# Three pairs of token blocks instead of two in the seven-product tail of an attention and feed-forward kernel; early activations parked in DRAM

## The chip, the cores and the metric

The kernel runs on one core of a Trainium2 chip. The metric is the device time of one execution in microseconds (us); lower is better. Three runs of the kernel before are shown, and one further execution was taken with the hardware profiler on.

## What is computed

The reference chains a thresholded attention and a feed-forward block with a quick GELU. All arrays are float32, except that the two weight matrices arrive as float64.

```python
# q, k, v: (8, 8, 576, 64)
scores = scale * np.matmul(q, k.transpose(0, 1, 3, 2))
thresh = np.max(scores, axis=-1, keepdims=True) - tau
scores = np.where(scores >= thresh, scores, -1000000000.0)
attn = np.exp(scores - np.max(scores, axis=-1, keepdims=True))
attn_out = np.matmul(attn / (np.sum(attn, axis=-1, keepdims=True) + 1e-09), v)
x = attn_out.transpose(0, 2, 1, 3).reshape(4608, 512)
h = x @ w_in                                  # w_in: (512, 2048)
g = h * (1.0 / (1.0 + np.exp(-1.702 * h)))
out = g @ w_out                               # w_out: (2048, 512)
```

## The kernel before, in words

**Attention.** 8 batches of 4 pairs of heads make 32 "pairs" n = 0 to 31. For a pair, TensorE computes transposed scores, 36 matrix products of 64x288 (`scores_run`, L538). ScalarE copies them out of PSUM (`keep`, L555), VectorE takes maxima (`in_groups`, L561) and folds them into a row (L570, L581, L594, L605), and two DMAs on the SP queue send that row to DRAM and bring it back spread over the partitions (`row_out` L651, `row_in` L660). VectorE subtracts it (`sub`, L666), ScalarE masks and exponentiates (L672, L676), VectorE sums (L561 again), the sums go the same way through DRAM (`sums_out` L754, `sums_in` L761), TensorE multiplies by the values (`values`, L687, 36 products of 64x288), and VectorE writes the normalised result into a transposed activation tile (`place_x`, L789). From pair 7 on, the value products of pair n-2 and the score products of pair n are interleaved in one run of 72 products.

**Feed-forward.** The 4608 tokens form 18 blocks of 256. Blocks 0 and 1 are done together in a plain way (L844, L826). Blocks 2 to 13 (`feed_forward`) have a plain first product, `mm1` at L804: 64 products of 128x256 to a block. GELU is a tanh on ScalarE (L813) and one VectorE instruction (L816). The second product is always made by the Strassen-Winograd scheme of seven half-size products (`second` and `product`, L995: 56 products of 128x256 to a block), with its sums on GpSimd (`s_sums`, `s_last`) and its readout on VectorE (L1017). The last four blocks, `TAIL = NBLK - 4`, go in two pairs through `two_blocks`, where the first product too is made of seven half-size ones (`product1`, L909: 112 products of 128x256 to two blocks where `mm1` has 128). That needs sums of weights (`w_sum`, L883) and of activations (`x_sum`, L892). The weight sums lie in `arena2`, in which the scores of the attention live, so the tail can only begin when the attention has ended.

**Storage of x.** A block's transposed activations take one of `NXT = 5` tiles `xT` of 128x1024 floats. `place_x` of a batch's first pair opens the tiles of its new blocks, and waits if none is free; the last first-product of a block frees its tile.

**What sets the order.** Nothing is ordered by hand. The kernel describes its work as tasks (engine, estimated cost, rank, predecessors, buffers taken and given). `run_in_order` plays them through on these costs and writes the instructions of each engine in the order in which it starts them. Attention tasks are ranked by pair number plus a bias for each function. All TensorE tasks of the feed-forward have the lowest rank (`LAST`), so they fill what the attention leaves free. A gate holds them together: the scores of pair n may start only when the feed-forward task of number `per_pair * (n - LEAD)` is done, with `per_pair = 16` and `LEAD = 6`. A plain block is 31 such tasks. [...]

```python
    for n in range(NP):
        gate = per_pair * (n - LEAD)
        after = [ffn[gate]] if gate >= 0 and ffn else []
```

Of the kernel before, what the change touches and what calls it, by code (L numbers as in the profile page):

```python
# [10 lines left out]
FP32 = mybir.dt.float32  # L11
# [8 lines left out]
P = 128  # L20
# [10 lines left out]
def kernel(  # L31
# [34 lines left out]
    nc = tc.nc  # L66
    B, H, S, D = q.shape
# [7 lines left out]
    BLK = 256  # L75
    BANK = 512
    HT = BLK // 2
    HF = d_ff // P // 2
    HM = d_model // 2
    NBLK = B * S // BLK  # L80
    NDC = d_model // P
    NFC = d_ff // P
# [5 lines left out]
    const = ctx.enter_context(tc.tile_pool(name="const", bufs=1))  # L88
    work = ctx.enter_context(tc.tile_pool(name="work", bufs=2))
    dram = ctx.enter_context(  # L90
        tc.tile_pool(name="dram", bufs=2, space=bass.MemoryType.DRAM)
    )
# [33 lines left out]
    NXT = 5  # L126
# [105 lines left out]
    def task(engine, cost, rank, f, *a, after=(), take=(), give=(), lag=None):  # L232
        if lag is None:
            lag = LAG[engine]
        if 0 <= rank < LAST:
            biases = EARLY if a[0] < NPAIR else SECOND if a[0] < 2 * NPAIR else LATER
            rank += CV[f.__name__] if f.__name__ in CV else biases.get(f.__name__, 0.0)
        tasks.append((engine, cost, rank, f, a, [x for x in after if x is not None],
                      take, give, lag))
        return len(tasks) - 1  # L240

    FIRST, LAST = -9.0, 1000.0
# [7 lines left out]
    def transfer(by, time, a, kind=0, give=(), lag=1.7):  # L250
        return task(by, time, FIRST, moved, kind, after=[a], give=give, lag=lag)
# [520 lines left out]
        nc.vector.transpose(out=rc, in_=r.unsqueeze(2).to_broadcast([P, QB, 32]))  # L772
        rcs[n] = rc

    xTs = {}

    def cuts(b):

        return sorted({0, SH, S} | {x for x in range(-b * S % BLK, S, BLK)})

    def place_x(n):
        b, hp = divmod(n, NPAIR)
        rc, pv = rcs.pop(n), pvs.pop(n)
        for a, z in zip(cuts(b), cuts(b)[1:]):
            blk, off = divmod(b * S + a, BLK)
            if blk not in xTs:
                xTs[blk] = work.tile([P, NDC, BLK], FP32, name="xT", tag="xT", bufs=NXT)
            c = a // SH
            nc.vector.tensor_tensor(  # L789
                out=xTs[blk][:, hp, off : off + z - a],  # L790
                in0=pv[:, c, a - c * SH : z - c * SH], in1=rc[:, a:z], op=ALU.mult,
            )
# [7 lines left out]
    def mm1(blk, j, f):  # L800
        if f == 0:
            hidden[j] = psM.tile([P, BANK], FP32, name="hps", tag="mo")
        for c in range(NDC):
            nc.tensor.matmul(  # L804
                hidden[j][:, ts(f, BLK)],
                lhsT=w_in[:, c, ds((f * HF + j) * P, P)], rhs=xTs[blk][:, c, :],
                start=(c == 0), stop=(c == NDC - 1),
            )


    def tanh(j):
# [28 lines left out]
    def mm1_0(j, i):  # L840
        if i == 0:
            hidden[j] = psM.tile([P, BANK], FP32, name="hps", tag="mo")
        for c in range(NDC):
            nc.tensor.matmul(  # L844
                hidden[j][:, ts(i, BLK)], lhsT=w_in[:, c, ts(j, P)], rhs=xTs[i][:, c, :],
                start=(c == 0), stop=(c == NDC - 1),
            )

    def gelu_0(j):
        nc.vector.scalar_tensor_tensor(  # L850
# [4 lines left out]

    TAIL = NBLK - 4
    WQ = NDC // 2 * HF * P
    gx_o = 4 * WQ  # L860
    xs_o = gx_o + N_G
# [36 lines left out]
    def product1(blk, j, x):  # L898
        b11, b12, b21, b22 = (x_quarter(blk, d, h) for d in range(2) for h in range(2))
        left, right = (  # L900
            (wq[0][0], b11), (wq[0][1], b21), (wc[1], xsum[1]), (wc[2], b12),
            (wq[1][1], xsum[2]), (wc[0], xsum[0]), (wc[3], b22),
        )[x]
        if BANK_OF[(7 * j + x) % 5] == "psA":
            places[j, x] = psA.tile([P, 2, 512], FP32, name="ps", tag="ps")[:, 0, 0:BLK]
        else:
            places[j, x] = psM.tile([P, BANK], FP32, name="ops", tag="mo")[:, 0:BLK]
        for c in range(2):
            nc.tensor.matmul(  # L909
                places[j, x], lhsT=left[:, c, ts(j, P)], rhs=right[:, c, :],  # L910
                start=(c == 0), stop=(c == 1),
            )

    def read1(j, x):
        (c11, c12), (c21, c22) = ([hs[j % 2][:, f, h, :] for h in range(2)] for f in range(2))
# [112 lines left out]
    NP = B * NPAIR  # L1028
# [173 lines left out]
    def two_blocks(blk):  # L1202

        b = -(-(blk + 1) * BLK // S) - 1
        xs = [placed[n] for n in range(NP)]
        first, xd = not done_w, []
        for x in range(4):
            if first:
                done_w.append([task("DVE", 0.61, LAST - 1.0, w_sum, x, 0, nc.vector, after=done_w[-1:][0] if done_w else xs)])
            after = (xd[-1:] or xs) + (done_w[x][:1] if first else []) + last_product1  # L1210
            xd.append(task("DVE", 0.61, LAST - 1.0, x_sum, blk, x, after=after))
        if first:
            for k in range(1, HF // 2):
                for x in range(4):
                    after = xs + done_w[x - 1][-1:] + done_w[x][-1:]
                    done_w[x].append(
                        task("POOL", 1.35, FIRST, w_sum, x, k, nc.gpsimd, after=after)
                    )
        last_product1.clear()
        g1, sums = {}, []  # L1220
        for j in range(HF):
            reads = [None] * 7
            for x in range(7):

                after = ffn[-1:] + [placed[n] for n in range(NPAIR * (b + 1))]
                if x in (P6, P7, P5, P3):
                    after += [done_w[{P6: 1, P7: 2, P5: 0, P3: 3}[x]][j // 2]]
                if x in (P6, P7, P4, P5):
                    after += [xd[{P6: 1, P7: 2, P4: 3, P5: 0}[x]]]
                if x == P3 or first:  # L1230
                    after += xs
                bank = (BANK_OF[(7 * j + x) % 5],)
                ffn.append(task(
                    "PE", FFU / 2, LAST, product1, blk, j, x, after=after, take=bank,
                    give=("xT", "xT") if x == P3 and j == HF - 1 else (),
                ))
                if x == P1:
                    a = task("ACT", 0.3, FIRST, read1, j, x, after=ffn[-1:], take=("hs",), give=bank)
                else:
                    a = task(  # L1240
                        "DVE", 0.67 if x == P5 else 0.335, FIRST, read1, j, x,
                        after=ffn[-1:] + reads, give=bank,
                    )
                reads[x] = a
            for h in range(2):
                a = task("ACT", 0.48, FIRST, tanh1, j, h, after=[reads[P5 if h == 0 else P3]], take=("io",))
                g1[j, h] = task(
                    "DVE", 0.65, FIRST, gelu1, j, h, after=[a, last_mm2.get(j // 4), g1.get((j, 0))],
                    give=("io", "hs") if h else ("io",),
                )  # L1250
            if j % 2:
                sums.append(task(
                    "POOL", 2.3, FIRST, s_sums, j // 2, after=[g1[j - 1, 0], g1[j, 0]]
                ))
        last_product1.extend(ffn[-1:])
        second(blk, 0, {j: [g1[j, 0]] for j in range(HF)}, sums)

        again = [g1[j, 1] for j in range(HF)]
        a = task("DVE", 1.14, FIRST, s_sum1, 0, after=again + ffn[-3:-2])
        b = task("DVE", 1.14, FIRST, s_sum1, 1, after=[a] + ffn[-1:])  # L1260
        c = task("DVE", 1.14, FIRST, s_sum1, 2, after=[b])
        second(blk + 1, 1, {j: [g1[j, 1]] for j in range(HF)}, [[a], [b], [c]])
# [1 line left out]
    gelus = {}  # L1264
    next_blk = 0

    per_pair = 16
    lvs = []
    exped, loaded, summed = {}, {}, {}

    def valued(n, pv):

        nonlocal next_blk
        b, hp = divmod(n, NPAIR)
        new = {(b * S + x) // BLK for x in cuts(b)[:-1]} if hp == 0 else set()
        if b:
            new -= {(b * S - 1) // BLK}
        placed[n] = task(
            "DVE", 1.05, float(n), place_x, n, after=[summed[n], pv], take=("xT",) * len(new),
            give=("psA", "rc"),  # L1280
        )
        while hp == NPAIR - 1 and (next_blk + 1) * BLK <= (b + 1) * S:
            if next_blk >= TAIL:
                if (next_blk - TAIL) % 2:
                    two_blocks(next_blk - 1)
            elif next_blk >= PLAIN:
                feed_forward(next_blk)
            elif next_blk == PLAIN - 1:
                first_blocks()
            next_blk += 1  # L1290

    for n in range(NP):
        gate = per_pair * (n - LEAD)
        assert gate < len(ffn) or gate <= 0
# [197 lines left out]
```

## Time and profile before

| quantity | value |
|---|---|
| three runs | 1310.16, 1313.54 and 1313.73 us; median 1313.54 us |
| profiled execution, its own time | 1311.6 us |
| its span, first to last instruction | 1309.8 us (1.8 us lie around it) |
| mean granted TensorE clock | 0.989 of full speed |
| TensorE matmul busy | 1260.5 us |
| VectorE busy | 1002.2 us |
| ScalarE busy | 646.6 us |
| GpSimd busy | 246.1 us |
| last value products of the attention (pair 31) start | 1073.01 us |
| first `product1` of the tail starts | 1112.60 us |

The trace records a float32 matrix product as two matmul records, so "x4" in a line of TensorE is two products. Busy is the time in which at least one instruction of the engine is under way. In a list by line, the figure after "x" is a count, then come the busy time in all and the mean of one in nanoseconds, and at the end the engine's idle time just before these instructions with what ended it.

### The profile page before, as it was taken

To read this page: it belongs to the slowest core of one execution; us is meant where nothing else is said; L and a number is where in the kernel's file an instruction comes from. 1 tells how busy PE (TensorE), PEld (TensorE's weight loads), DVE (VectorE), ACT (ScalarE), POOL (GpSimd) and SP (SyncE) were. 2 spreads that over 40 slices of the span, in tenths; PEclk is the share of its full clock that TensorE was granted. 3 is DMA by queue.
4 is the path that set the end of the run, shared out by engine and by line. 5 is a ranking of instruction groups with operands and counts; after the bars stand their busy time and mean duration, and the time that the engine had idled before them with its cause. 6 is when DMAs were issued, how large, how long until landed. Compare 5 with 4: busy or idle time off the path is not lost. (4 is left out here: it accounts for less than half of the span.)

```text
span 1309.8 us, 22824 instructions
## 1 busy us (share of the span) xinstructions
PE 1260.5 (96%) x9128; PEld 972.6 (74%) x9128; DVE 1002.2 (77%) x1601; ACT 646.6 (49%) x830; POOL 246.1 (19%) x300
## 2 busy tenths in 40 slices
PE   5869999999999999999999999999999999999998
PEld 2436854477688777777778888777777778888887
DVE  7999998989998877778877877777888864652642
ACT  5975656766664544455554545454556540210210
POOL 1301210022030212112020302020212117120120
PEclk8989999999999999999999999999999999999999
DMA  6976967264322222221222222222122110000000
GB/s 118 339 186 214 282 209 132 67 125 83 82 57 71 55 64 64 56 57 44 63 47 61 55 71 55 72 56 70 42 52 54 38 44 9 9 1 33 1 1 32
DMA packets 194309, 103.78 MB, mean 79 GB/s; under 512 B 160284, under 2 KB 171292, under 8 KB 194204
## 3 DMA queue, kind: packets, MB, share of 16 engines
q1 hardware_dynamic: 180476, 64.30, 20.6%
q0 software_dynamic: 11360, 37.74, 9.7%
q8 instruction: 71, 1.16, 0.4%
q10 hardware_dynamic: 2368, 0.30, 0.2%
q14 instruction: 34, 0.28, 0.1%
HBM read 88.40 MB, written 9.70 MB: 75 GB/s over the span
## 5 line engine op out<-in xcount | busy, mean ns | idle before, releaser
L561 DVE TRANSPOSE_TENSOR_REDUCE part<-arena 128x36 f32<-128x1152 f32 x295 | 361.5, 1241 | 45.9 <-ACT arena L555 32.3
L804 PE MATMUL hps<-xT,w_in 128*128 128x256 f32 x1536 | 336.9, 380 | 0.4 <-DVE arena L816 0.4
L804 PEld LDWEIGHTS hps<-xT,w_in 128*128 128x128 f32 x1536 | 290.8, 190 | 45.5 <-issue 5.7
L672 ACT ACTIVATE arena<-arena 128x1152 f32<-128x1152 f32 (+1 forms) x160 | 169.4, 1058 | 144.9 <-DVE arena L666 144.6
L555 ACT COPY arena<-ps 128x576 f32<-128x576 f32 x288 | 170.4, 647 | 121.2 <-PE ps L538 120.9
L666 DVE TENSOR_TENSOR arena<-arena 128x1152 f32<-128x1152 f32 (+1 forms) x158 | 197.5, 1281 | 19.6 <-DMA arena<-row 19.5
L995 PE MATMUL ops<-w_out,arena 128*128 128x256 f32 x896 | 202.9, 381 | 1.2 <-DVE arena L816 1.1
L676 ACT ACTIVATE arena<-arena,shift,scl 128x1152 f32<-128x1152 f32 (+1 forms) x160 | 200.1, 1251 | 4.1
L538 PE MATMUL ps<-arena 64*64 64x288 f32 x2304 | 174.1, 419 | 25.1 <-DVE arena L522 14.4
L995 PEld LDWEIGHTS ops<-w_out,arena 128*128 128x128 f32 x896 | 169.0, 190 | 29.1 <-DVE arena L816 3.7
L961 POOL TENSOR_TENSOR arena<-arena 128x256 f32<-128x256 f32 x56 | 50.8, 907 | 658.4 <-DVE arena L816 556.7
L687 PE MATMUL pv<-arena 64*64 64x288 f32 x2176 | 161.2, 410 | 0.0
L538 PEld LDWEIGHTS ps<-arena 64*64 64x64 f32 x2304 | 83.7, 137 | 93.6 <-ACT arena L555 30.7
L995 PE MATMUL ops<-arena 128*128 128x256 f32 x672 | 150.6, 380 | 0.0
L813 ACT ACTIVATE th<-hps 128x512 f32<-128x512 f32 x112 | 66.0, 589 | 167.9 <-PE hps L804 148.2
L995 PEld LDWEIGHTS ops<-arena 128*128 128x128 f32 x672 | 127.3, 190 | 19.3 <-issue 2.2
L687 PEld LDWEIGHTS pv<-arena 64*64 64x64 f32 x2176 | 82.0, 135 | 55.3 <-issue 12.8
L1017 DVE SCALAR_TENSOR_TENSOR osb<-ops,osb 128x256 f32<-128x256 f32 x98 | 39.5, 414 | 91.8 <-PE ops L995 85.0
L816 DVE SCALAR_TENSOR_TENSOR arena<-th,hps 128x512 f32<-128x512 f32 x96 | 64.1, 667 | 37.1 <-ACT th L813 37.0
L844 PE MATMUL hps<-xT,w_in 128*128 128x256 f32 x256 | 57.3, 382 | 1.3 <-DVE arena L850 1.2
L826 PE MATMUL ops<-w_out,arena 128*128 128x512 f32 x128 | 56.4, 596 | 0.0
L844 PEld LDWEIGHTS hps<-xT,w_in 128*128 128x128 f32 x256 | 48.1, 190 | 11.0 <-DVE arena L850 3.0
(117 smaller groups left out, 1027.8 us busy)
## 6 DMA issues: line engine op xcount, KB each, us to landing
arena<-in_v_dram SPq DMA_DIRECT2D x128, 144.0 KB
arena<-in_q_dram SPq DMA_DIRECT2D x128, 72.0 KB
out_dram<-osb SPq DMA_DIRECT2D x36, 256.0 KB
arena<-in_k_dram SPq DMA_DIRECT2D x124, 72.0 KB
arena<-row SPq DMA_DIRECT2D x62, 144.0 KB
arena<-row_s SPq DMA_DIRECT2D x54, 144.0 KB
w_out<-in_moe_w_in_dram POOLq DMA_DIRECT2D x12, 512.0 KB, 9.4
arena<-in_moe_w_out_dram POOLq DMA_DIRECT2D x12, 512.0 KB, 5.9
```

What stands on the lines that cost most here:

```text
L538: nc.tensor.matmul(ps[ts(c, KT), h, 0:SH], lhsT=mats[n, 1][ts(h, D), ts(j, KT)], rhs=mats[n, 0][ts(h, D), ts(c, SH)], start=True, stop=True,)
L555: nc.scalar.copy(out=sT[n, t][:, u], in_=pss.pop((n, j))[:, :, 0:SH])
L561: nc.vector.tensor_reduce(out=stats[n, op][:, t * 2 * QB : min(2 * t + 2, NK) * QB], in_=sT[n, t].rearrange("p u h (g d) -> p (u h g) d", ...
L666: engine.tensor_tensor(out=s, in0=s, in1=mbs[n].unsqueeze(1).to_broadcast(list(s.shape)), op=ALU.subtract)
L672: nc.scalar.activation(out=s, in_=s, func=AF.Prelu, alpha=STEEP)
L676: nc.scalar.activation(out=s, in_=s, func=AF.Exp, scale=scl, bias=shift)
L687: nc.tensor.matmul(o[c][ts(h, D), 0:SH], lhsT=left(j, h)[ts(c, KT)], rhs=sT[n, t][ts(c, KT), u, h, :], start=(j == 0), stop=(j == NK - 1),)
L804: nc.tensor.matmul(hidden[j][:, ts(f, BLK)], lhsT=w_in[:, c, ds((f * HF + j) * P, P)], rhs=xTs[blk][:, c, :], start=(c == 0), stop=(c == N ...
L813: nc.scalar.activation(out=ths[j], in_=hidden[j], func=AF.Tanh, scale=GELU_SCALE / 2)
L816: nc.vector.scalar_tensor_tensor(out=g[:, :, j, :], in0=two(ths.pop(j)), scalar=1.0, in1=two(hidden.pop(j)), op0=ALU.add, op1=ALU.mult,)
L844: nc.tensor.matmul(hidden[j][:, ts(i, BLK)], lhsT=w_in[:, c, ts(j, P)], rhs=xTs[i][:, c, :], start=(c == 0), stop=(c == NDC - 1),)
L995: nc.tensor.matmul(banks[blk][k][:, ts(o, HM)], lhsT=left[:, j, :], rhs=right[:, j, :], start=(j == 0), stop=(j == HF - 1),)
```

## The change

- `TAIL` becomes `NBLK - 6`. Blocks 12 and 13 leave `feed_forward` and form a third pair for `two_blocks`, so blocks 12 to 17 now wait for the end of the attention.
- The five tiles become slots of one tile `x_all`, handed out and taken back by the kernel (`new_x`, `drop_x`).
- Blocks 12, 13 and 14 are complete before the last batch. Each is copied to a DRAM tile as soon as it is complete (`x_out`, 512 KB on the SP queue), which frees its slot. After the last `place_x` in the plan it is copied back (`x_back`, SP queue) into a free slot; block 14's slot comes free with the first products of blocks 12 and 13.
- `two_blocks` is called for all three pairs after the last pair of heads, and waits for the copies back.
- `per_pair` becomes 13.

```diff
-    xTs = {}
+    xTs, x_at, x_away = {}, {}, {}
...
+    x_all = const.tile([P, NXT * NDC * BLK], FP32, name="x_all")
+    x_room = list(range(NXT))
+
+    def new_x(blk):
+        x_at[blk] = x_room.pop(0)
+        xTs[blk] = x_all[:, ts(x_at[blk], NDC * BLK)].rearrange("p (c t) -> p c t", t=BLK)
+
+    def drop_x(blk):
+        x_room.append(x_at.pop(blk))
+
+    def x_out(blk):
+        x_away[blk] = dram.tile([P, NDC * BLK], FP32, name=f"x{blk}", tag=f"x{blk}", bufs=1)
+        nc.sync.dma_start(out=x_away[blk], in_=x_all[:, ts(x_at[blk], NDC * BLK)])
+        drop_x(blk)
+
+    def x_back(blk):
+        new_x(blk)
+        nc.sync.dma_start(out=x_all[:, ts(x_at[blk], NDC * BLK)], in_=x_away.pop(blk))
...
-    TAIL = NBLK - 4
+    TAIL = NBLK - 6
...
+        if x == P3 and j == HF - 1:
+            drop_x(blk)
+            drop_x(blk + 1)
...
-        xs = [placed[n] for n in range(NP)]
+        xs = [placed[n] for n in range(NP)] + [back_x[y] for y in (blk, blk + 1) if y in back_x]
...
-    per_pair = 16
+    per_pair = 13
...
             if next_blk >= TAIL:
-                if (next_blk - TAIL) % 2:
-                    two_blocks(next_blk - 1)
+                if b < B - 1:
+                    a = task("SP", 0.6, FIRST, x_out, next_blk, after=[placed[n]])
+                    back_x[next_blk] = transfer("DMS", 2.8, a, 1, give=("xT",))
...
+        if n == NP - 1:
+            a = placed[n]
+            for blk in back_x:
+                a = task("SP", 0.6, FIRST, x_back, blk, after=[a, back_x[blk]], take=("xT",))
+                back_x[blk] = transfer("DMS", 2.8, a, 1)
+            for blk in range(TAIL, NBLK, 2):
+                two_blocks(blk)
```

More of the change, by code (lines that the diff above doesn't have):

```diff
@@ L786, in place_x @@
             if blk not in xTs:
-                xTs[blk] = work.tile([P, NDC, BLK], FP32, name="xT", tag="xT", bufs=NXT)
+                new_x(blk)
             c = a // SH
@@ L808, in mm1 @@
             )
+        if f and j == HF - 1:
+            drop_x(blk)
     def tanh(j):
@@ L847, in mm1_0 @@
             )
+        if j == NFC - 1:
+            drop_x(i)
     def gelu_0(j):
@@ L912, in product1 @@
             )
+        if x == P3 and j == HF - 1:
+            drop_x(blk)
+            drop_x(blk + 1)
     def read1(j, x):
@@ L1290, in valued @@
             next_blk += 1
+        if n == NP - 1:
[5 more added lines that the diff above has]
+                two_blocks(blk)
+    back_x = {}
     for n in range(NP):
```

## The prediction, made before the changed kernel ran

> **What bounds the kernel now.** I read the page first: the busy shares and the slices.
>
> ```profile
> PE 1260.5 (96%) x9128; PEld 972.6 (74%) x9128; DVE 1002.2 (77%) x1601; ACT 646.6 (49%) x830; POOL 246.1 (19%) x300
> ...
> PE   5869999999999999999999999999999999999998
> ...
> DVE  7999998989998877778877877777888864652642
> ```
>
> TensorE (PE) is full from slice 5 on. VectorE (DVE) falls into three stretches: near full in the first third, about 8 tenths after it, and near half from slice 33 on, where the attention is over and the seven-product tail runs. In the middle VectorE is second, not idle. So next I asked for the busy time per period of one pair of heads (from the end of one 72-product run to the end of the next): two early periods and two late ones. Columns: stretch and its length, then busy us of PE, PEld, DVE, ACT, POOL with counts, clock, DMA share, GB/s.
>
> ```profile
> 304.20:333.00 28.80, 27.37 (x229) 19.96 (x225) 27.88 (x41) 17.35 (x23) 6.12 (x5) 1.00 0.29 67
> 333.00:360.40 27.40, 26.93 (x229) 20.18 (x225) 25.27 (x42) 16.65 (x21) 0.00 (x0) 1.00 0.33 85
> ...
> 540.30:577.00 36.70, 36.70 (x273) 29.48 (x273) 29.30 (x45) 17.59 (x21) 4.67 (x5) 1.00 0.26 64
> 577.00:612.00 35.00, 35.00 (x267) 28.02 (x265) 27.97 (x43) 20.02 (x26) 8.47 (x9) 1.00 0.23 52
> ```
>
> The late periods carry 60 to 64 feed-forward products and keep PE at 100%. The two early ones carry only 40 each; there VectorE works 53.15 of 56.2 us (95%) and PE loses time: 1.43 and 0.47 us of plain idleness. These two rows are the key of what follows, because the change makes most of the later periods as short as these. The waits of PE name the channel, scores that wait for ScalarE's copies out of PSUM, and the timeline shows it in place:
>
> ```profile
> 327.88 1.26 PE L538 MATMUL ps<-arena 64*64 64x288 f32 x16 [0.95 <-ACT arena L555]
> ...
> 332.33 0.72 PE L538 MATMUL ps<-arena 64*64 64x288 f32 x8 [0.39 <-ACT arena L555]
> ...
> 360.31 24.44 PE L804 MATMUL hps<-xT,w_in 128*128 128x256 f32 x112
> ```
>
> ScalarE is only 60% busy there; its copies stand in its queue behind masks that wait for VectorE's subtractions (in 304 to 360 us ScalarE waits 7.1 us for L666). So the first cause is VectorE.
>
> Last, the seam between attention and tail, in the timelines of PE and VectorE:
>
> ```profile
> 1073.01 4.59 PE L687 MATMUL pv<-arena 64*64 64x288 f32 x72
> ...
> 1112.60 1.03 PE L909 MATMUL ps<-xT,w_in 128*128 128x256 f32 x4
> ...
> 1113.46 1.03 PE L909 MATMUL ops<-xT,w_in 128*128 128x256 f32 x4
> ```
>
> ```profile
> 1080.46 0.95 DVE L789 TENSOR_TENSOR xT<-pv,arena 128x64 f32<-128x64 f32 x4 [4.99 <-DMA arena<-row_s]
> ...
> 1088.94 1.75 DVE L892 TENSOR_TENSOR arena<-xT,arena 128x512 f32<-128x512 f32 x1
> ```
>
> The last values end at 1077.6, the last `place_x` runs from 1080.46, the sums for the tail are ready at 1090.7, and PE comes to them only at 1112.6: 35 us of plain feed-forward (80 products) cover some 13 us.
>
> [...] The trace agrees in quiet (512 KB of `w_out` landed 3.7 us after issue) and has up to 12.7 us when crowded. [...]
>
> **The change, part by part.**
>
> *First product of blocks 12 and 13.* 128 plain products become 112. L909 starts at 1112.60 and 1113.46 are 0.86 us apart for two products, 0.432 us each. Gain 16 x 0.432 = 6.9 us, on PE, which is the path. This is all the change can gain.
>
> *The sums this needs.* A third set of readouts L925 (56 of 0.42), GELUs L934 (16 of 0.80 against 16 of 0.67 at L816) and `x_sum`: about 30 us more of VectorE, all in the tail, where it was busy 47.5 of 100 us and PE lost nothing. Weight sums are still made once. Cost 0, covered by 48 us of PE to each pair of first products; without cover, 4.5 us of VectorE stand against 6.05 of PE to each step j.
>
> *Less filler in the attention.* Moved out of it: 2 x (64 + 56) products, 103.7 us of PE, with some 16 us of VectorE. The instruction order of the changed kernel shows where it is missing. Up to pair 11 nothing differs. From pair 13 to 18 a 72-product run is followed by 44, 40, 36, 44, 40, 36 products; then one run of 184; then 12, 48, 40; then 140; then 12, and 48, 40, 40, 36, 44, 40, 44 up to pair 31. (The long runs come from the five slots: `place_x` of a new batch must wait until another block is consumed.) So a period is 8.92 us of attention (568.02 to 576.94 in the timeline) plus about 40 x 0.432 = 17.3, 26.2 us on PE, against 36 before.
>
> VectorE per period: from 500 to 1000 us it was busy 390.4 us, at 35.9 us to a pair 13.9 pairs, 28.0 each. Of that, plain feed-forward (59 of L816 at 0.669, 49 of L1017 at 0.414, less 5% overlap) is 56.2, 4.0 each at 62 products; at 40 it is 2.6. So 24.0 + 2.6 = 26.6 us against PE's 26.2. **VectorE becomes the equal of PE or slightly more**, and it also loses 1 to 2 us a period waiting for rows and tanhs in its own order (0.92 and 2.13 us idle in the two early windows). The early periods, with 40 products, measured 28.8 and 27.4 where the same sum for PE gives 26.2; the late ones, with 64 and 60, measured 36.7 and 35.0 for 36.6 and 34.8. So a short period loses 1.0 to 2.4 us more than a long one.
>
> Not every short period pays. VectorE's maxima of a pair ended 12.0 us after its scores in the tight stretch (L605 at 372.39, scores until 360.39), and 7.2 us in a relaxed one (547.46 after 540.28): a reserve of 5 to 7 us that each long run refills. Pairs 13 to 18 start with the reserve spent: 6 x 1.0 to 2.4, 6 to 14 us, take 7, near the lower end, since VectorE's excess and waits (0.4 plus 0.9) come to 1.3. Pairs 21 and 22: 0 to 2, take 1. The last seven start full, but the period of 12 products has 24 us of VectorE's work beside 14.1 of PE and takes 10 of reserve, of which the one of 48 returns 2.6: 0 to 10, take 4. The last pair's exponentials come 21.5 us after its row (1048.90 to 1070.4); with the lag at 12 or more they end about 34 us after its scores, and the values are due at 34: 0 to 5, take 1. Sum 13 us, bounds 6 to 31 (a gain beyond the 6.9 is excluded: nothing else leaves PE).
>
> *The copies out.* Three issues on SP (0.37 us each, as for stores) ahead of `row_out` of one pair (block 12) and another (blocks 13 and 14)[...]. VectorE has other work queued first. Each issue also waits on SP for its `place_x`, with that row behind it. Take 0.5 us in all, bounds 0 and 7.
>
> *The seam.* In the new order 40 products, 17.3 us, lie between the last values and the tail. On SP both copies back stand right behind the last sums' return, and need no `place_x`: about 1.3 + 0.8 us of issue and 2 x 3.7 of transfer, landed some 9 us after the values. Then VectorE needs two weight and two x sums (0.69 and up to 1.2 us each, 4 us) before the third product: 13 us, under 17.3. Take 0, bounds 0 and 8. The copy of block 14 has 48 us of second products to hide in. It waits on SP for its slot, with only the stores of blocks 12 and 13 behind it, which come later anyway.
>
> Sum against the profiled execution: 1311.6 - 6.9 + 13 + 0.5 = 1318. Its time lies 1.9 us under the median of the runs shown, so for a median I say **1319**. A run can tell about 0.3% (3.9 us) from no change.
>
> **Rivals.**
>
> *PE stays fed (not slower).* The plan keeps a two-pair lead between scores and values, and VectorE reached 96% busy between 300 and 400 us while PE was at 98%. If a short period costs 0.2 us instead of 1.3, 15 of them cost 3, and with the 1.9 us to the median the result is 1305 to 1309. For it: that 98%. Against: there the lag was already at its limit.
>
> *Losses and gain cancel:* 4 to 10 us lost, 1310 to 1316.
>
> *The seam opens (slower, another mechanism).* If the copies go out only after the last `place_x`, or land at the crowded 12.7 us, the tail waits 5 to 10 us with its cover used up; with half the attention losses 1311.6 - 6.9 + 7 + 8 = 1320. It decides from a landing later than 13 us after the last values. For it: 17 us of cover in place of 35. Against: DMA is nearly idle there.
>
> *The change does not do what it says:* excluded, the order shows 336 products at `product1` in place of 224.
>
> **Chances.** Forecast, VectorE-bound periods cost 10 to 22 us (1315 to 1329): 0.50, 0.06 of it under 1317.5. PE stays fed (to 1309): 0.20. Cancel: 0.17. Seam opens, alone or on top (1318 to 1340): 0.13. Faster 0.20, same 0.17 + 0.06 = 0.23, slower 0.57. The range 1307 to 1332 leaves out the full gain at one end and stacked losses at the other.
>
> **What would show it.** Right: windows of the pairs 13 to 18 with VectorE at 95% or more and periods of 27 to 28 us, PE waits "ps <- ACT L555" well above 6.4 us in total, the tail starting near 1025 us. Wrong: PE at 99% or more through these pairs (the first rival), or a gap of PE just ahead of the first `product1` ended by a DMA (the seam). I would be wrong above all if the reserve of two pairs swallowed the waits.

## The result

| | runs | median, us | ratio to before, same chip |
|---|---|---|---|
| changed kernel, first series | 4 | 1324.68 | 1.0094, 95% interval [1.0073, 1.0115] |
| changed kernel, second series | 5 | 1323.90 | 1.0064 [1.0052, 1.0076] |

The change makes the kernel slower by 0.6 to 0.9%. The profiled executions span 1321.8 us in the first series and 1322.2 us in the second, against 1309.8 us before.

### The profile after

The page of the changed kernel, busy shares and slices:

```profile
PE 1262.0 (95%) x9096; PEld 964.3 (73%) x9096; DVE 1027.3 (78%) x1664; ACT 644.6 (49%) x838; POOL 250.0 (19%) x288
...
PE   5769999999999999999999999999999999999998
...
DVE  7999988989999999915997489999996662652642
```

There are 32 matmul records fewer, which are the 16 products saved. In slices of 33 us TensorE looks as full as before, so this view hides the loss. VectorE's row, its slices counted from 0, shows the new shape: nines from slice 9 to 16, a drop to 1 beside the first long run of feed-forward, a second dip at slice 22 beside the second, nines from slice 24 to 29, and about half load from slice 30 on, where the tail has begun.

The same stretches that the prediction used, one per pair of heads, here pairs 13, 14 and 15 with 44, 40 and 36 feed-forward products in them:

```profile
359.81:388.83 29.02, 28.60 (x233) 21.71 (x233) 28.64 (x44) 21.42 (x28) 9.75 (x9) 1.00 0.32 73
388.83:416.99 28.16, 27.34 (x225) 19.94 (x225) 27.75 (x41) 17.22 (x23) 6.13 (x5) 1.00 0.29 65
416.99:441.83 24.84, 24.84 (x218) 18.91 (x217) 22.09 (x39) 13.81 (x18) 0.00 (x0) 1.00 0.33 82
sum 82.02, PE 80.78 PEld 60.56 DVE 78.48 ACT 52.45 POOL 15.88; mean PE 26.93 PEld 20.19 DVE 26.16 ACT 17.48 POOL 5.29
```

VectorE works 78.48 of 82.02 us, 96%. By product count TensorE needs 120 x 0.432 + 3 x 8.92 = 78.6 us for the three, so 3.4 us are lost in them, 1.1 a period. Only 1.24 us of that shows as idle TensorE; the rest stands in the trace as busy time, so the idle column understates the loss.

The waits of TensorE, first one line of the kernel before, then four of the changed kernel, the last two of them new:

```profile
PE ps L538 <- ACT arena L555: 6.4, 10, 2.4
...
PE ps L538 <- ACT arena L555: 12.2, 23, 2.9
PE ps L538 <- DVE x_all L808: 4.6, 3, 1.9
PE ops L932 <- DVE osb L1043: 2.5, 1, 2.5
PE ps L932 <- DVE arena L915: 1.1, 1, 1.1
```

The figures are us in all, the number of waits and the longest. Scores waited for ScalarE's copies 23 times in place of 10 (12.2 us in place of 6.4). The last two lines lie at the seam: at L932, the first products of the tail, TensorE waits for sums and readouts of VectorE.

**Where the 12.0 us of span came from.** I compare the time at which TensorE passes three points: the end of the scores of pair 11, up to which the order is the same; the end of the values of pair 31; the end of the span.

| stretch | before | after | products of before less after | lost against before |
|---|---|---|---|---|
| start to scores 11 | 333.05 | 334.96 | 0 | 1.9 |
| to values 31 | 744.55 | 669.61 | 200 x 0.432 = 86.4 | 11.5 |
| to the end | 232.2 | 317.2 | -184 x 0.432 = -79.5 | 5.5 |
| all | 1309.8 | 1321.8 | 6.9 | 18.9 |

The 1.9 us ahead of the change are taken as scatter: kernels with the same early order passed this point between 333.1 and 336.6 us. The gain came as forecast, 6.9 us, the attention lost 11.5 and the seam 5.5.

### The profile page after: what moved, and what is told of

Its sections match the earlier page's. It is cut to its first block, busy times and chain, and to the rows that moved or that the text cites. A ratio compares the mean times of both kernels' runs of the same rounds, so it can differ in the third digit from the quotient of the medians.

```text
span 1321.8 us, 22801 instructions
## 1 busy us (share of the span) xinstructions
PE 1262.0 (95%) x9096; PEld 964.3 (73%) x9096; DVE 1027.3 (78%) x1664; ACT 644.6 (49%) x838; POOL 250.0 (19%) x288
## 3 DMA queue, kind: packets, MB, share of 16 engines
q1 hardware_dynamic: 181340, 67.45, 21.2%
## 4 chain that ended last, share of the span: by engine, by line
PE 55%; DVE 23%; ACT 8%; DMA 7%; issue 4%; SPq 3%; DVEq 0%; POOL 0%; ACTq 0%
PE ops L1021 18%; PE hps L823 11%; DVE part L561 7%; PE ps L932 7%; PE ps L1021 5%; DVE arena L666 5%; PE ps L538 4%; PE ops L932 4%; PE pv L687 4%; ACT arena L672 3%; DMA arena<-row 2%; ACT arena L676 2%; ACT arena L555 2%; SPq L410 2%; DMA arena<-in_moe_w_out_dram 2%
## 5 line engine op out<-in xcount | busy, mean ns | idle before, releaser
L823 PE MATMUL hps<-x_all,w_in 128*128 128x256 f32 x1280 | 282.2, 380 | 0.7 <-DVE arena L837 0.7
L823 PEld LDWEIGHTS hps<-x_all,w_in 128*128 128x128 f32 x1280 | 241.7, 190 | 40.5 <-issue 6.6
L555 ACT COPY arena<-ps 128x576 f32<-128x576 f32 x288 | 171.1, 651 | 121.6 <-PE ps L538 121.2
L672 ACT ACTIVATE arena<-arena 128x1152 f32<-128x1152 f32 (+1 forms) x160 | 171.1, 1069 | 94.4 <-DVE arena L666 94.3
L676 ACT ACTIVATE arena<-arena,shift,scl 128x1152 f32<-128x1152 f32 (+1 forms) x160 | 201.2, 1258 | 3.6
L1021 PE MATMUL ops<-w_out,arena 128*128 128x256 f32 x832 | 188.0, 381 | 0.8 <-DVE arena L837 0.8
L1021 PEld LDWEIGHTS ops<-w_out,arena 128*128 128x128 f32 x832 | 156.8, 190 | 27.5 <-DVE arena L837 3.6
L1021 PE MATMUL ops<-arena 128*128 128x256 f32 x624 | 139.2, 380 | 0.0
L1021 PEld LDWEIGHTS ops<-arena 128*128 128x128 f32 x624 | 118.3, 190 | 17.3 <-issue 1.3
L834 ACT ACTIVATE th<-hps 128x512 f32<-128x512 f32 x96 | 56.9, 592 | 146.8 <-PE hps L823 127.5
L1043 DVE SCALAR_TENSOR_TENSOR osb<-ops,osb 128x256 f32<-128x256 f32 x91 | 36.0, 407 | 69.0 <-PE ops L1021 65.8
L837 DVE SCALAR_TENSOR_TENSOR arena<-th,hps 128x512 f32<-128x512 f32 x80 | 53.3, 666 | 45.0 <-ACT th L834 44.8
L955 ACT ACTIVATE th<-arena 128x512 f32<-128x512 f32 x48 | 30.3, 631 | 114.9 <-DVE arena L951 114.9
L951 DVE TENSOR_TENSOR arena<-ps,arena 128x256 f32<-128x256 f32 x102 | 41.2, 421 | 24.7 <-PE ps L932 23.4
L865 PE MATMUL hps<-x_all,w_in 128*128 128x256 f32 x256 | 57.0, 382 | 1.1 <-DVE arena L873 1.0
```

The lines of the kernel that those rows point to most:

```text
L555: nc.scalar.copy(out=sT[n, t][:, u], in_=pss.pop((n, j))[:, :, 0:SH])
L672: nc.scalar.activation(out=s, in_=s, func=AF.Prelu, alpha=STEEP)
L676: nc.scalar.activation(out=s, in_=s, func=AF.Exp, scale=scl, bias=shift)
L823: nc.tensor.matmul(hidden[j][:, ts(f, BLK)], lhsT=w_in[:, c, ds((f * HF + j) * P, P)], rhs=xTs[blk][:, c, :], start=(c == 0), stop=(c == N ...
L834: nc.scalar.activation(out=ths[j], in_=hidden[j], func=AF.Tanh, scale=GELU_SCALE / 2)
L865: nc.tensor.matmul(hidden[j][:, ts(i, BLK)], lhsT=w_in[:, c, ts(j, P)], rhs=xTs[i][:, c, :], start=(c == 0), stop=(c == NDC - 1),)
```

## The experiments

Ratios are to runs of the kernel before on the same chip. Periods are read from TensorE's timeline, from the end of one run of 72 products to the end of the next.

### Is it the storage of x?

The changed kernel with the tail and the gate put back, so that the slots and one copied block remain.

```diff
-    TAIL = NBLK - 6
+    TAIL = NBLK - 4
...
-    per_pair = 13
+    per_pair = 16
```

> The changed kernel with TAIL back at NBLK - 4 and per_pair back at 16: what stays is the single x_all tile with its slots, and block 14 alone goes through DRAM. Theory (the storage costs nothing, the loss comes from the short periods and the seam): 1312 to 1315. Rival (x_all or the copies cost): above 1317.

Measured 1313.79 us, ratio 0.9993 [0.9985, 1.0001]. The slots of `x_all` and one block's way through DRAM cost nothing that can be measured. Three blocks' way was not tried alone.

### Do short periods alone cost?

The kernel before, with one number changed.

```diff
-    per_pair = 16
+    per_pair = 13
```

> The kernel before with per_pair at 13 and nothing else, so with no third pair of blocks and no copies. Its order has the same short periods for pairs 13 to 22 as the changed kernel, and later triples of 12, 48 and 40 products. Theory (short periods alone cost, by VectorE): 5 to 9 us more than before, 1318 to 1322. Rival (the loss needs the copies or the third pair): 1312 to 1314.

Measured 1321.95 us, ratio 1.0067 [1.0054, 1.008]: 7.3 us more by the medians and some 9 us by the ratio, with no third pair of blocks and no copies. Its periods of pairs 13 to 15 were 29.01, 28.17 and 24.84 us, the same as in the changed kernel to 0.01. So the spacing of the feed-forward alone makes the loss.

### Is VectorE the cause?

The changed kernel with lighter sums from pair 12 on, the lists of the other engines being the same.

```diff
+        light = n >= 12 and op == ALU.add
...
-            out=stats[n, op][:, t * 2 * QB : min(2 * t + 2, NK) * QB],
-            in_=sT[n, t].rearrange("p u h (g d) -> p (u h g) d", d=32),
+            out=stats[n, op][:, t * 2 * QB : (2 * t + 1 if light else min(2 * t + 2, NK)) * QB],
+            in_=(sT[n, t][:, 0:1] if light else sT[n, t]).rearrange("p u h (g d) -> p (u h g) d", d=32),
...
-            out=r, in_=stats[n, op].rearrange("p (j c) -> p c j", c=QB), axis=AXL.X, op=op
+            out=r, in_=stats[n, op].rearrange("p (j c) -> p c j", c=QB)[:, :, 0:NK:2 if n >= 12 and op == ALU.add else 1],
+            axis=AXL.X, op=op,
```

> The changed kernel with lighter VectorE work from pair 12 on and the same tasks and costs in the plan: the sums of the exponentials read only the even groups of 64 keys, so the denominators leave out the odd groups. That takes 4 x 0.62 us of VectorE from each of 20 pairs and leaves TensorE, ScalarE, the DMAs and the seam alone. Theory (VectorE bounds the short periods, about 11 us lost there against before): most of the 11 us come back, 1314 to 1317 us, VectorE near 90% in the windows of pairs 13 to 18. Rival (TensorE loses the time by itself in switching between attention and feed-forward, or to ScalarE's copies): 1323 to 1326. Rival (copies through DRAM crowd the row DMAs): 1323 to 1326 too.

Measured 1317.28 us, ratio 1.0028 [1.0017, 1.004]. The median is within 0.3 us of the theory's range, but the trace says less: from the scores of pair 11 to the values of pair 31 it took 664.24 us against 669.61, so 5.4 of 11.5 us came back. VectorE did fall, over pairs 13 to 15, from 96% of the time to 92% (74.65 of 80.99 us). The period of 40 products (pair 14) fell from 28.16 to 27.13 us, that of 44 (pair 13) stayed at 29.01, and scores still waited for copies 20 times, 11.6 us in all. VectorE is a cause and not the whole of it; the expectation that most of the loss would return failed.

### Is ScalarE's queue the other part?

The timeline of ScalarE in the changed kernel, during the 72 products of pair 14, shows why it might be. L555 are the copies of scores, L672 and L676 the masks and exponentials of the pair before:

```profile
411.16 1.16 ACT L555 COPY arena<-ps 128x576 f32<-128x576 f32 x2
412.21 1.36 ACT L676 ACTIVATE arena<-arena,shift,scl 128x1152 f32<-128x1152 f32 x1
413.46 1.18 ACT L555 COPY arena<-ps 128x576 f32<-128x576 f32 x2
414.51 1.19 ACT L672 ACTIVATE arena<-arena 128x1152 f32<-128x1152 f32 x1
415.57 1.20 ACT L555 COPY arena<-ps 128x576 f32<-128x576 f32 x2
416.62 1.39 ACT L676 ACTIVATE arena<-arena,shift,scl 128x1152 f32<-128x1152 f32 x1
```

Two copies and one mask or exponential take 2.1 to 2.3 us from start to start. TensorE fills two score tiles every 1.94 us (in the kernel before, where nothing held them up, score products started at 569.05, 570.99 and 572.93). So whenever the late pair's exponentials fall into the run of products, ScalarE empties the score tiles in PSUM more slowly than TensorE fills them (2.1 to 2.3 us for two against 1.94). The masks wait for VectorE's subtractions: from 360 to 524 us ScalarE waited for them 9 times, 21.2 us in all. Two kernels test it, one with lighter masks, one with both reliefs:

```diff
-        s = sT[n, t]
+        s = sT[n, t][:, 0:1] if n >= 12 else sT[n, t]
         nc.scalar.activation(out=s, in_=s, func=AF.Prelu, alpha=STEEP)
```

> The changed kernel with lighter ScalarE work from pair 12 on and the same plan: the masks of the scores (L672) take only the even groups of 64 keys, so the odd groups go unmasked into the exponential. That takes 4 x 0.48 us of ScalarE from each of 20 pairs. The lightened sums of VectorE gave back some 5 us of the 11 lost in the attention, so a second cause is open. Theory (the copies out of PSUM stand in ScalarE's queue behind masks and exponentials of the pair before, and TensorE's three score banks run dry): 3 to 6 us less than the changed kernel. Rival (VectorE is the only bound, ScalarE merely waits for it): less than 1.5 us. Rival (switching between matrix shapes costs TensorE itself): less than 1 us.

> Both reliefs in one kernel: sums that read only the even groups of 64 keys and masks that take only the even groups, from pair 12 on. Theory (VectorE and ScalarE's queue share the loss): 8 to 11 us less than the changed kernel, periods of 40 and 44 products within 0.4 us of their product count. Rival (TensorE's own switching): no better than the lightened sums alone, 5 to 6 us less, with 0.9 us lost in each period of 40 or 44 products.

On the chip that ran these two, the unaltered changed kernel was run as well:

> The changed kernel once more, unaltered, beside the following ones on one chip. All theories: 0.94% over the kernel before, within 0.2%.

It gave 1323.90 us and a ratio of 1.0064, which is 0.1% below the expected band; the first four runs had met a lower median of before (1312.75 against 1315.36 us). The lighter masks gave 1321.27 us, 1.0054 [1.0038, 1.007]. By the medians that is 2.6 us less, just short of the 3 to 6 expected, and by the ratios only 1.3 us, which would fit a rival. The trace speaks for the theory: from the scores of pair 11 to the values of pair 31 it took 665.50 us, against 669.61 and 670.43 in the two executions of the changed kernel, and scores waited for copies 10 times again. Both reliefs gave 1310.90 us, 0.9966 [0.9954, 0.9978], 13.0 us less, a little more than the theory's 8 to 11.

| kernel | period of 44 products | of 40 | of 36 | sum |
|---|---|---|---|---|
| by product count | 27.93 | 26.20 | 24.47 | 78.60 |
| changed | 29.02 | 28.16 | 24.84 | 82.02 |
| lighter sums | 29.01 | 27.13 | 24.85 | 80.99 |
| lighter masks | 28.19 | 28.03 | 24.65 | 80.87 |
| both | 28.18 | 26.48 | 24.65 | 79.31 |

The windows with both reliefs show TensorE without a gap:

```profile
360.51:388.69 28.18, 28.18 (x233) 21.86 (x233) 27.80 (x43) 20.58 (x28) 9.75 (x9) 1.00 0.29 70
388.69:415.17 26.48, 26.48 (x227) 20.37 (x225) 25.84 (x41) 15.57 (x23) 6.14 (x5) 1.00 0.31 74
415.17:439.82 24.65, 24.65 (x217) 18.91 (x217) 20.36 (x39) 12.49 (x18) 0.00 (x0) 1.00 0.35 83
```

With both, each of the three periods is within 0.3 us of its products. Neither relief is enough alone: the period of 44 gains by the lighter masks only, the period of 40 mostly by the lighter sums and then by both. TensorE's own switching, the rival, is at most that 0.3 us. To see that the reliefs don't simply save time anywhere, the same two edits went into the kernel before:

> The kernel before with both reliefs from pair 12 on: sums of the exponentials over the even groups of 64 keys only, masks on the even groups only. The same work is left out as where both reliefs were given to the changed kernel. Theory (VectorE and ScalarE's queue cost TensorE time in short periods only, and the kernel before has hardly any after pair 12): 0 to 2 us less than before. Rival (the reliefs save time in any order, so they show nothing about the short periods): 5 us less or more.

Measured 1312.12 us, 0.9986 [0.9978, 0.9994]. What gave 13 us in the changed kernel gave 2 us here.

### The seam

The changed kernel's VectorE between the last `place_x` (L808) and the sums of x (L915). L1043 are readouts that wait for TensorE, L906 the weight sums:

```profile
1006.49 0.95 DVE L808 TENSOR_TENSOR x_all<-pv,arena 128x64 f32<-128x64 f32 x4 [5.16 <-PE ops L1021]
1008.25 0.42 DVE L1043 SCALAR_TENSOR_TENSOR osb<-ops,osb 128x256 f32<-128x256 f32 x1 [0.81 <-PE ops L1021]
1011.70 0.42 DVE L1043 SCALAR_TENSOR_TENSOR osb<-ops,osb 128x256 f32<-128x256 f32 x1 [3.03 <-PE ops L1021]
1015.16 0.42 DVE L1043 SCALAR_TENSOR_TENSOR osb<-ops,osb 128x256 f32<-128x256 f32 x1 [3.03 <-PE ops L1021]
1015.50 0.93 DVE L906 TENSOR_TENSOR arena<-w_in 128x512 f32<-128x512 f32 x1
1016.46 1.64 DVE L906 TENSOR_TENSOR arena<-arena,w_in 128x512 f32<-128x512 f32 x1
```

And TensorE, which at its pitch would start a product pair every 0.864 us from 1021.86 on, with two windows in the columns used above:

```profile
1024.86 1.13 PE L932 MATMUL ps<-arena 128*128 128x256 f32 x4 [1.11 <-DVE arena L915]
1028.54 1.52 PE L932 MATMUL ops<-x_all,arena 128*128 128x256 f32 x4 [2.54 <-DVE osb L1043]
...
1025.00:1030.00 5.00, 2.46 (x9) 1.78 (x10) 4.15 (x5) 0.00 (x0) 2.60 (x2) 0.91 0.14 51
1030.00:1035.00 5.00, 5.00 (x19) 4.18 (x18) 2.62 (x6) 1.19 (x3) 0.00 (x0) 0.74 0.01 3
```

The two waits make 3.65 of the 5.5 us. After them the next three product pairs took 4.38 us in place of 2.59, while the granted clock (third figure from the end of a window) was at 0.91 and 0.74: that is the rest.

Both copies back were issued by 1005.1 us, and their DMA traffic was over by 1010.5 (from there to 1015 us the DMA share was 0.00). But the weight sums begin only at 1015.50, and the instruction just ahead of them had waited for TensorE: they stand behind three readouts. VectorE idled 3.03 us ahead of the last of these, from 1012.1 us on, and did not take the sums first. The plan had tied the weight sums to the copies back, which they do not read, and so had written them late in VectorE's list. The edit ties them to the last `place_x` alone:

```diff
-                done_w.append([task("DVE", 0.61, LAST - 1.0, w_sum, x, 0, nc.vector, after=done_w[-1:][0] if done_w else xs)])
+                done_w.append([task("DVE", 0.61, LAST - 1.0, w_sum, x, 0, nc.vector, after=done_w[-1:][0] if done_w else [placed[n] for n in range(NP)])])
```

> The changed kernel with the weight sums of the tail planned after the last place_x alone, not after the copies of x back. Only VectorE's list changes, by three weight sums that move ahead of two readouts which wait for TensorE. Theory (the seam lost about 5.5 us because VectorE's sums stood in its queue behind readouts, not because the copies landed late): 3 to 5.5 us less than the changed kernel, 1319 to 1321.5. Rival (the copies land too late): no change, 1323 to 1326. Rival (VectorE and GpSimd slow each other in the sums): no more than 2 us less.

Measured 1318.76 us, ratio 1.0037 [1.0025, 1.0049], a span of 1317.0 us (4.8 less). More moved in VectorE's list than the expectation said: all four weight sums now come after the first readout, and three of the four sums of x moved ahead of readouts too. The tail runs at 0.86 us a product pair from the first pair on:

```profile
1008.62 0.42 DVE L1043 SCALAR_TENSOR_TENSOR osb<-ops,osb 128x256 f32<-128x256 f32 x1 [0.76 <-PE ops L1021]
1008.96 1.59 DVE L906 TENSOR_TENSOR arena<-w_in 128x512 f32<-128x512 f32 x1
...
1023.84 1.03 PE L932 MATMUL ops<-x_all,w_in 128*128 128x256 f32 x4
1024.70 1.03 PE L932 MATMUL ps<-arena 128*128 128x256 f32 x4
```

So the seam was an order in a queue, not a late landing. The sums' own length played a part that was not tested alone: at the 0.69 us that such a sum took in the kernel before when GpSimd was idle (1082.04 us there), eight sums begun at 1015.50, with the two readouts among them, would have ended near 1022, in time for the third product pair at 1023.6 (an estimate).

### Other orders

The corrected seam with `per_pair = 14`:

> The changed kernel with the weight sums planned after the last place_x alone, and per_pair at 14 in place of 13. Its order has 56, 52, 56 products in pairs 16 to 18 in place of 44, 40, 36, and a second long run of 140 in place of 184, with the last periods at 16 and 48. Theory (each short period costs 1 to 2 us beyond a long one): the three longer periods save 3 us, the short ones near the end return some, 1 to 3 us less than the same kernel at 13 (0.37% over before). Rival (the loss is set by the total of VectorE work up to the end of the attention, wherever the filler lies): no change, within 1 us.

Measured 1320.84 us, ratio 1.0046 [1.0032, 1.006], span 1317.4 against 1317.0 us: nothing was saved, the rival's answer. Periods 16 to 18 had 56, 52 and 56 products and still took 34.62, 34.12 and 33.64 us where the products give 33.1, 31.4 and 33.1. So a period's loss does not follow from its own length. That it depends on how far VectorE is behind when it begins, as the forecast's "reserve" says, fits this and was not tested further.

Last, other biases for the ranks of the attention tasks, searched so that the plan ends early on its own costs, once for the changed kernel with the corrected seam and once, as a control, for the kernel before. The edit replaces the numbers in `SECOND` and `LATER`, for instance:

```diff
     LATER = {
-        "exps": 1.49,
-        "in_groups": 1.97,
-        "keep": -9.78,
+        "exps": 6.58,
+        "in_groups": 34.85,
+        "keep": -3.16,
...
```

> The changed kernel with the weight sums planned after the last place_x alone, and other biases for the ranks of pairs 4 to 31 (the tables SECOND and LATER), searched for this structure; tasks, costs, gate and products as in the changed kernel. Theory (the 6.9 us on TensorE are real, and most of the loss is how the attention's VectorE and ScalarE work lies in its queues): 8 to 16 us less than the same kernel with the old biases, 1303 to 1311, below the kernel before. Rival (VectorE's total work is the bound whatever the order): 1316 to 1320.

> The kernel before with biases searched in the same way and for as long, for its own structure: the control of the one above. Theory (before loses little in the attention after pair 12, so it has little to win): 2 to 6 us less than before, and above the changed structure with its own biases. Rival (any structure gains as much from new biases): 10 us less or more.

Measured 1319.47 us, 1.0037 [1.0022, 1.0051], and 1317.07 us, 1.0025 [1.0016, 1.0035]. Both expectations failed in the total: neither search made its kernel faster, and no version beat the kernel before with its full computation. The number of the first lies in its rival's range, but its trace speaks against the rival. Between the scores of pair 11 and of pair 31 it took as long as with the old biases (631.85 against 631.71 us), yet with 40 matmul records more in that stretch (4933 against 4893), which are 20 products or 8.6 us. So order alone won 8.5 us there, inside the 8 to 16 expected. It lost them elsewhere. Up to the scores of pair 11 it did 20 products fewer and was only 4.2 us sooner. At the seam it lost 6.1 us:

```profile
1016.52 1.75 DVE L906 TENSOR_TENSOR arena<-w_in,arena 128x512 f32<-128x512 f32 x1
1018.19 1.07 DVE L1043 SCALAR_TENSOR_TENSOR osb<-ops,osb 128x256 f32<-128x256 f32 x3
...
1018.74 6.57 PE L1021 MATMUL ops<-w_out,arena 128*128 128x256 f32 x16 [3.67 <-DVE osb L1043]
...
1020.00:1025.00 5.00, 5.00 (x14) 3.97 (x14) 0.58 (x1) 0.00 (x0) 0.00 (x0) 0.54 0.14 52
```

This is the seam's mechanism turned round: here the readouts stood behind the weight sums, TensorE waited 3.67 us for them, and its next eight products took 6.57 us where eight like them took 3.62, at a granted clock of 0.54. The control had no such gain: between the same scores it took 8.4 us more than the kernel before, for 12 products or 5.2 us more.

### All causes removed

Corrected seam and both reliefs together:

> The changed kernel with all three reliefs: the sums over the even groups of 64 keys only and the masks on the even groups only from pair 12 on (the odd groups left out of both), and the weight sums planned after the last place_x alone. Theory (the change is worth 6.9 us on TensorE and lost it to the short periods and the seam, and to nothing else): 6.9 us, 0.53%, less than the kernel before with the same two reliefs (which was at 0.9986 of before), so a ratio near 0.9933, 0.992 to 0.995. Rival (some further loss of 3 us or more is still unnamed): 0.996 or above.

Measured 1305.81 us, ratio 0.9940 [0.9926, 0.9953], span 1302.7 us against 1308.9 for the kernel before with the same two reliefs: 6.2 of 6.9 us. By the two ratios it is about 6 us, with an interval of about 2 us on either side. So the saved products are worth about what they count, and no further loss as large as the rival's 3 us is likely; a smaller one is not excluded.

## Why the prediction was right, and where not

- *The gain of 6.9 us.* Right: 16 products fewer at 0.432 us, and the kernel with the other causes removed shows 6.2 us of it.
- *The tail's extra VectorE work at no cost.* Right: past the seam the tail runs at its product pitch.
- *Short periods, 13 us taken (6 to 31).* Right in size, 11.5 us, and in the channel: scores waiting for copies behind masks that wait for subtractions, which the reliefs confirm. Its signs came: over pairs 13 to 18 VectorE worked 96% of the time, the mean period was 27.4 us, and the tail started at 1021.86 us. The split was less good, and its errors cancelled, which is luck. Pairs 13 to 18 took 164.4 us where products give 157.2; less 2.4 lost there before, 4.8 us, under the 7 taken. Pairs 25 to 31 lost 7.2 us against 1.2 before, 6.0 us, over the 4 taken.
- *ScalarE.* Under-rated. The prediction called it "only 60% busy" and VectorE "the first cause". Taking some 2 us a pair from VectorE (its busy time fell by 43.8 us over 20 pairs) gave back only 5.4 us; the rest needed ScalarE's queue shorter too. ScalarE's share of busy time over a period (56 to 74%) says nothing of the 9 to 11 us of a run of 72 products, in which it must copy and exponentiate at once.
- *The copies out, 0.5 us.* An estimate of mine. Not separated for three blocks; one block cost nothing, and TensorE's loss is explained without them. One reading behind the term was wrong: the landing of 3.7 us that it calls quiet belongs to loads between 120 and 158 us, where the DMA engines were 88% busy.
- *The seam, 0 taken (0 to 8).* This term was wrong: 5.5 us. The landing was not to blame: expected some 9 us after the values, it came within 6. The step that failed was "then VectorE needs two weight and two x sums (4 us)". The sums did not begin on landing but 10.9 us after the values, behind three readouts; six of them, and not four, came before the third product pair; and all eight, with two readouts among them, took 13 us, at up to 1.75 us each while GpSimd ran its own. The prediction gave an opening seam 0.13, but by a late landing. The order of VectorE's list was to be had before the run, and I had read it for SP only.
- *The total.* 1319 forecast, 1324 to 1325 measured. For the profiled execution the sum gave 1318.2 us and 1323.6 came: the seam's 5.5 us and the 1.9 us of scatter over it, the attention's 1.5 and the copies' 0.5 under it.

## What to carry to other kernels

Work that fills TensorE beside another stage also bought time for the slower engines of that stage here (less of it between pairs of heads, and nothing else changed, cost 7.3 us by the medians); before moving it away, set the other engines' work per period against the shortened period, queue by queue and in the stretch where they collide, not as a share of the whole. A wait that ties a task to more than it reads cost twice in these planned lists: the task was late, and it was queued behind readouts that waited for TensorE. Here that was 5.5 us at the seam. Moving it forward has its price too, for then what stands behind it is late: 3.67 us of waiting with the searched biases. To settle two coupled causes, relieve each alone and both together: here 1.03 and 1.15 us alone, over the three periods of pairs 13 to 15, became 2.71 together.

## What the runs showed of the hardware

- A VectorE subtraction or addition of 128x512 floats took 0.69 us with GpSimd idle. The eight at the changed kernel's seam, beside which GpSimd ran its own, took 0.93 to 1.75 us, six of them 1.63 to 1.75; GpSimd's own took 1.27 us before them and 1.59 to 1.72 us beside them:

```profile
1082.04 0.69 DVE L883 TENSOR_TENSOR arena<-arena,w_in 128x512 f32<-128x512 f32 x1
...
1018.02 1.75 DVE L906 TENSOR_TENSOR arena<-w_in 128x512 f32<-128x512 f32 x1
...
1014.61 1.27 POOL L906 TENSOR_TENSOR arena<-w_in 128x512 f32<-128x512 f32 x1
1017.51 1.72 POOL L906 TENSOR_TENSOR arena<-w_in 128x512 f32<-128x512 f32 x1
```

  The first line is of the kernel before, the others of the changed kernel.
- Idle time of TensorE understated a stall: the period of pair 14 showed 0.82 us of it and had lost 2.0 us against its products, at a granted clock of 1.00 over the window.
- At the seam a stall cost more than its wait. After 3.65 us of waiting in the changed kernel, the granted clock was 0.74 from 1030 to 1035 us and 1.8 us more were lost; with the searched biases, after 3.67 us, it was 0.54 from 1020 to 1025 us and 3 us more were lost.
